# Segment sums by small TensorE products instead of VectorE reductions, and an attention transpose by VectorE and GpSimd

## The chip, the core and the metric

The kernel runs on one core of a Trainium2 chip. A core has five engines that run side by side, each with its own list of instructions: TensorE (PE in the profile) multiplies matrices from SBUF into PSUM, VectorE (DVE), ScalarE (ACT) and GpSimd (POOL) work elementwise, and SyncE (SP) issues transfers. PEld is TensorE's loading of weights, which overlaps its matmuls. The metric is the time of one execution on the device in microseconds; of several runs the median is given.

## The reference, cut to what matters

Two blocks are computed from the same normalised input `xn` and added. Block A is attention in segments of 32 tokens with 8 memory tokens carried from segment to segment. Block B is a mixer and a large MLP.

```python
def _A_ref(x, mem0, Wq, Wk, Wv, Wo, seg_len):      # S 2048, Dm 1024, H 32, Dh 128, M 8, seg_len 32
    mem = mem0
    for s in range(n_seg):                          # 64 segments
        h = concatenate([mem, x[:, s*32:(s+1)*32]], axis=1)      # 40 tokens
        q, k, v = h @ Wq, h @ Wk, h @ Wv
        p = softmax(where(mask, q @ k.T * scale, -1e9))          # the memory sees all, a token the past
        o = (p @ v) @ Wo
        mem = o[:, :M]
        outs.append(o[:, M:])

def _B_ref(x, w1, w2, w3, w4):
    h = gelu(layernorm(x) @ w1)
    x1 = x + shifted(h) @ w2
    return x1 + gelu(layernorm(x1) @ w3) @ w4       # 1024 -> 3584 -> 1024

xn = layernorm(x)
return x + _A_ref(xn, ...) + _B_ref(xn, ...)
```

The kernel does not run the 64 segments one after the other. It takes the memory that a segment passes on from the mean of the 40 value rows of that segment (put through `Wv` and `Wo`), attends to it for all segments at once, and checks at the end that the true memory is close enough to the one taken; a slow exact branch stands by in case it isn't. For that mean the kernel needs **the sum of `xn` over each segment of 32 tokens**, for all 64 segments: the tile `xs`, later `xb` in bf16. The first segment, whose memory is the input `mem0`, gets an attention of its own with all 40 rows: 40 queries by 40 keys, four heads at a time, eight times.

## The kernel before, the parts that are touched

Order of the stages: layernorm and the product with `w1` (stage 1), the product with `w2`, the MLP with `w3` and `w4` in four blocks `tb` of 512 tokens, the attention in 32 steps (four blocks of 512 tokens by eight groups of four heads), each with 12 chains of eight matmuls for Q, K and V, and the output product. All engines' orders are written down by hand: each engine runs its instructions in the order of the program. Products of 512 columns go to one of four rotating PSUM buffers (tag "mm").

Stage 1, where every tile of 128 tokens is normalised in place:

```python
def normalise_x(n):
    nc.scalar.activation(xts[n][:], xts[n][:], ACTF.Identity, bias=nms.pop(n)[:], scale=lnst[:, n, 2:3])   # L245
...
for g in range(2, NT // 2):
    ...                                             # statistics, normalised copy, its DMA transpose, for g+1
    stage1(g, range(4))                             # 4 x 8 matmuls of 256 columns, L260
    for n in (2 * g, 2 * g + 1):
        normalise_x(n)
    stage1(g, range(4, KT))
```

The MLP stage. `filler` puts side work into it: in `prep` the segment sums, in `plan` the 16 chunks of `Wv` and `Wo` through which the sums pass:

```python
plan = {}
for i in range(4):
    plan[(1, 1, 2 * i + 1)] = i
    plan[(2, 0, 7 * i + 6)] = 4 + i
    plan[(2, 1, 2 * i + 1)] = 8 + i
    plan[(3, 0, 7 * i + 6)] = 12 + i

def make_xn(n):                                     # normalised x once more, to memory
    xt = ring.tile([P, D], BF16, tag="xt", name="xt", bufs=2)
    nc.sync.dma_start(xt[:], x_v[:, n, :])
    nc.vector.tensor_scalar(xt[:], xt[:], ..., op0=ALU.subtract, op1=ALU.mult)                             # L455
    nc.gpsimd.dma_start(xn_v[:, n, :], xt[:])                                                              # L456

def load_sum(b):                                    # 512 tokens, transposed on the way in
    sums[b] = x3_pool.tile([P, KT * 512], BF16, tag="x0", name=f"xTs{b}")
    nc.sync.dma_start_transpose(sums[b]..., xn_d[b * 512:(b + 1) * 512, :])                                # L460

def seg_sums(b, k0):
    nc.vector.tensor_reduce(xs[:, k0:k0 + 2, ...], sums[b]..., axis=AX.X, op=ALU.add)                      # L463

for n in range(6):       do(0, 0, 10 + 3 * n, make_xn, n)
for n in range(6, 14):   do(0, 1, n - 6, make_xn, n)
do(1, 0, 0, make_xn, 14); do(1, 0, 3, make_xn, 15)
# load_sum and four seg_sums for each b: loads at (0,1,1) (0,1,5) (1,0,3) (1,0,14),
# sums at (0,1,4), (1,0,1) and (1,0,2), (1,0,10..13), (1,0,22..25); last_sum and load_chunk(0) at (1,0,26)

def load_R1(n):
    R1 = ring.tile([P, D], F32, tag="R1", name="R1")                    # three buffers
    nc.sync.dma_start(R1[:], R1_v[:, n, :])
    xt = ring.tile([P, D], BF16, tag="xt", name="xt", bufs=2)
    nc.sync.dma_start(xt[:], x_v[:, n, :])
    nc.gpsimd.tensor_tensor(R1[:], R1[:], xt[:], op=ALU.add)                                               # L509

for tb in range(4):
    for f in range(FT):                             # 28 chains of 8 matmuls
        ps = mm_tile("ps3")
        for k in range(KT):
            nc.tensor.matmul(ps[:], w3[...], xn3Ts[tb][:, :, k, :], ...)                                   # L580
        nc.scalar.activation(h3T[:, f, :], ps[:], ACTF.Gelu_apprx_tanh)
        filler(tb, 0, f)
        if f == 20:
            load_R1(tb * 4)
    for j in range(4):
        n = tb * 4 + j
        if j < 3:
            load_R1(n + 1)
        R1 = R1s.pop(n)
        for ch in range(2):
            ps = mm_tile("ps4")
            for f in range(FT):                     # 28 matmuls
                nc.tensor.matmul(ps[:], h3T[:, f, j * P:(j + 1) * P], w4t[f // 4][...], ...)               # L596
            nc.vector.tensor_tensor(R1[:, ch...], ps[:], R1[:, ch...], op=ALU.add)                         # L597
            filler(tb, 1, 2 * j + ch)
        nc.gpsimd.dma_start(R_v[:, n, :], R1[:])                                                           # L599
```

The first segment's attention, run once in each of the first eight steps. Its parts for step p are placed between the chains of the step after it: `first_scores` behind chain 4, `first_soft` behind chain 8, `first_trans` behind chain 11, and `first_values` behind chain 1 of the step after that:

```python
def first_soft(s):
    ...                                             # four matmuls psZ (L766), softmax on VectorE and ScalarE
    nc.vector.tensor_tensor(PZ[0:L, :, 0:L], e[:], mx..., op=ALU.mult)                                     # L775

def first_trans(s):
    ps = mm_tile("psZT")[:, 0:4 * L].rearrange("p (h k) -> p h k", h=4)
    for hh in range(4):
        nc.tensor.matmul(ps[:, hh, :], PZ[:, hh, :], ident[:, 0:L], start=True, stop=True)                 # L780
    s.PZT = smp.tile([P, 4, L], BF16, tag="PZT", name="PZT")
    nc.scalar.copy(s.PZT[:], ps)                                                                           # L782

def first_values(s):
    ps = mm_tile("psZO")[:, 0:4 * L].rearrange("p (h k) -> p h k", h=4)
    for hh in range(4):
        nc.tensor.matmul(ps[:, hh, :], VZ[:, hh * P:(hh + 1) * P], s.PZT[:, hh, :], start=True, stop=True) # L787
    nc.scalar.copy(oX[:, hsl(s.hg), 0:SEG], ps[:, :, 0:SEG])
    nc.scalar.copy(oZ[:, hsl(s.hg), :], ps[:, :, SEG:L])
```

Of the kernel before, what the change touches and what calls it, by code (L numbers as in the profile page):

```python
# [13 lines left out]
BF16 = mybir.dt.bfloat16  # L14
F32 = mybir.dt.float32
# [48 lines left out]
def kernel(  # L64
# [79 lines left out]
    xs = spec.tile([P, KT, NSEG], F32)  # L144
    xb = spec.tile([P, KT, NG], BF16)
    m0 = spec.tile([M, D], BF16)
    m0s = spec.tile([P, KT, 1], F32)
    lnst = spec.tile([P, NT, 4], F32)

    rightx = main.enter_context(ExitStack())  # L150
# [14 lines left out]
    with ExitStack() as keepx:  # L165
# [6 lines left out]
        with ExitStack() as p0:  # L172
# [71 lines left out]
            def normalise_x(n):  # L244
                nc.scalar.activation(xts[n][:], xts[n][:], ACTF.Identity, bias=nms.pop(n)[:], scale=lnst[:, n, 2:3])  # L245

            def pe_trans(n):
                xn2 = xn2s.pop(n)
                ps = [mm_tile("psT")[:], mm_tile("psT")[:]]
                for h in range(2):  # L250
# [3 lines left out]
                    for q in range(0, 4, 2 if n == 0 else 4):  # L254
                        w = 2 if n == 0 else 4
                        nc.scalar.copy(xn2Ts[n // 2][:, n % 2, 4 * h + q:4 * h + q + w, :], p3_[:, q:q + w, :])

            def w1_part(g, co, ps, ks):
                for k in ks:
                    nc.tensor.matmul(ps, w1_sb[:, k, co * P:(co + 1) * P], xn2Ts[g][:, :, k, :], start=(k == 0), stop=(k == KT - 1))  # L260
                if ks[-1] == KT - 1:
                    nc.scalar.activation(hTB[:, co, 2 + g * 256:2 + g * 256 + 256], ps, ACTF.Gelu_apprx_tanh)
# [58 lines left out]
            ln_apply(4)  # L321
            dma_trans(4)
            single(3, 0)
            normalise_x(2)
            ln_stats(6)
            ln_apply(5)
# [3 lines left out]
            for g in range(2, NT // 2):  # L330
                nxt = [n for n in (2 * g + 2, 2 * g + 3) if n < NT]
                for n in nxt:
                    if 6 < n + 1 < NT:
                        ln_stats(n + 1)
                    ln_apply(n)
                    dma_trans(n)
                stage1(g, range(4))
                for n in (2 * g, 2 * g + 1):
                    normalise_x(n)
                stage1(g, range(4, KT))  # L340

        x3_pool = rightx.enter_context(tc.tile_pool(name="x3", bufs=1, side="right"))
        w3b_pool = rightx.enter_context(tc.tile_pool(name="w3b", bufs=1, side="right"))
# [35 lines left out]
    with ExitStack() as p3:  # L379
# [9 lines left out]
        for k in range(KT):  # L389
            nc.tensor.matmul(ps9[:, k, :], m0[:, k * P:(k + 1) * P], eye9[:], start=True, stop=True)  # L390
        nc.vector.tensor_copy(MZ[:, :, 0:M], ps9[:, :, 0:M])
        nc.vector.tensor_copy(m0s[:], ps9[:, :, M:M + 1])

        chunks = {}

# [44 lines left out]
        plan = {}  # L440
        slots = {}
        for i in range(4):
            plan[(1, 1, 2 * i + 1)] = i
            plan[(2, 0, 7 * i + 6)] = 4 + i
            plan[(2, 1, 2 * i + 1)] = 8 + i
            plan[(3, 0, 7 * i + 6)] = 12 + i
        for c in range(16):
            slots[c] = 0 if c < 8 else c % 2

        sums = {}  # L450

        def make_xn(n):
            xt = ring.tile([P, D], BF16, tag="xt", name="xt", bufs=2)
            nc.sync.dma_start(xt[:], x_v[:, n, :])
            nc.vector.tensor_scalar(xt[:], xt[:], lnst[:, n, 0:1], lnst[:, n, 2:3], op0=ALU.subtract, op1=ALU.mult)  # L455
            nc.gpsimd.dma_start(xn_v[:, n, :], xt[:])  # L456

        def load_sum(b):
            sums[b] = x3_pool.tile([P, KT * 512], BF16, tag="x0", name=f"xTs{b}")
            nc.sync.dma_start_transpose(sums[b][:].rearrange("p (k t) -> p k t", k=KT), xn_d[b * 512:(b + 1) * 512, :])  # L460

        def seg_sums(b, k0):
            nc.vector.tensor_reduce(xs[:, k0:k0 + 2, 16 * b:16 * b + 16], sums[b][:].rearrange("p (k s i) -> p k s i", k=KT, i=SEG)[:, k0:k0 + 2, :, :], axis=AX.X, op=ALU.add)  # L463

        def last_sum():
            nc.vector.tensor_tensor(xb[:, :, 0:1], m0s[:], xs[:, :, 0:1], op=ALU.add)
            nc.vector.tensor_copy(xb[:, :, 1:NG], xs[:, :, 1:NG])
            load_chunk(0, 0)

        prep = {}  # L470

        def do(tb, ph, i, f, *a):
            prep.setdefault((tb, ph, i), []).append((f, a))

        for n in range(6):
            do(0, 0, 10 + 3 * n, make_xn, n)
        for n in range(6, 14):
            do(0, 1, n - 6, make_xn, n)
        do(1, 0, 0, make_xn, 14)
        do(1, 0, 3, make_xn, 15)  # L480
        for b, (load, sumat) in enumerate((((0, 1, 1), [(0, 1, 4)] * 4), ((0, 1, 5), [(1, 0, 1)] * 2 + [(1, 0, 2)] * 2),
                                           ((1, 0, 3), [(1, 0, 10 + t) for t in range(4)]), ((1, 0, 14), [(1, 0, 22 + t) for t in range(4)]))):
            do(*load, load_sum, b)
            for t, pos in enumerate(sumat):
                do(*pos, seg_sums, b, 2 * t)
        do(1, 0, 26, last_sum)

        def filler(tb, ph, i):
            for f, a in prep.get((tb, ph, i), ()):
                f(*a)  # L490
            c = plan.get((tb, ph, i))
            if c is None:
                return
            use_chunk(c)
            nx = c + 2 if c >= 8 else c + 1
            if c == 7:
                load_chunk(8, slots[8])
                load_chunk(9, slots[9])
            elif c < 7 or nx < 16:
                load_chunk(nx, slots[nx])  # L500
# [3 lines left out]
        def load_R1(n):  # L504
            R1 = ring.tile([P, D], F32, tag="R1", name="R1")
            nc.sync.dma_start(R1[:], R1_v[:, n, :])
            xt = ring.tile([P, D], BF16, tag="xt", name="xt", bufs=2)
            nc.sync.dma_start(xt[:], x_v[:, n, :])
            nc.gpsimd.tensor_tensor(R1[:], R1[:], xt[:], op=ALU.add)  # L509
            R1s[n] = R1  # L510

        A = {}
# [45 lines left out]
        def att_prep():  # L558
            load_xT(0)
            for nm in "qkv":  # L560
                need_w(nm, 0)
            need_w("q", 1)
            make_xm(0)
            sm = A["sm"]
            A["EQ"] = sm.tile([P, 16, W], F32, name="EQ")
            nc.gpsimd.memset(A["EQ"][:, :, SEG:W], float(M))
            for nm in ("QZ", "PZ", "VMZ"):
                A[nm] = sm.tile([P, 4, SEG if nm == "VMZ" else P], BF16, name=nm)
                nc.gpsimd.memset(A[nm][:], 0.0)
            A["VZ"] = sm.tile([P, 512], BF16, name="VZ")  # L570
            nc.gpsimd.memset(A["VZ"][:], 0.0)
            A["SS"] = sm.tile([P, 16], F32, name="SSsum")
            nc.gpsimd.memset(A["SS"][:], 0.0)

        for tb in range(4):
            for f in range(FT):
                ps = mm_tile("ps3")
                w3 = w3a if f < FH else w3b
                for k in range(KT):
                    nc.tensor.matmul(ps[:], w3[:, k, (f % FH) * P:(f % FH + 1) * P], xn3Ts[tb][:, :, k, :], start=(k == 0), stop=(k == KT - 1))  # L580
                nc.scalar.activation(h3T[:, f, :], ps[:], ACTF.Gelu_apprx_tanh)  # L581
                filler(tb, 0, f)
                if f == 20:
                    load_R1(tb * 4)
            if tb == 3:
                rightx.close()
                att_open()
# [7 lines that stand above are left out]
                    for f in range(FT):  # L595
                        nc.tensor.matmul(ps[:], h3T[:, f, j * P:(j + 1) * P], w4t[f // 4][:, f % 4, ch * 512:(ch + 1) * 512], start=(f == 0), stop=(f == FT - 1))  # L596
                    nc.vector.tensor_tensor(R1[:, ch * 512:(ch + 1) * 512], ps[:], R1[:, ch * 512:(ch + 1) * 512], op=ALU.add)  # L597
                    filler(tb, 1, 2 * j + ch)
                nc.gpsimd.dma_start(R_v[:, n, :], R1[:])  # L599
                if tb == 3 and j == 0:  # L600
                    att_prep()
# [143 lines left out]
                nc.scalar.copy(oT[:, h0:h0 + 4, :].rearrange("p h (m j) -> p m h j", j=4)[:, 0:3, :, 2 * r + j], o4[:, j, 0:12].rearrange("p (m h) -> p m h", h=4))  # L745
            nc.scalar.copy(oT[:, h0:h0 + 3, 12 + 2 * r:14 + 2 * r].rearrange("p h j -> p j h"), o4[:, :, 12:15])

    QZ, PZ, VMZ, VZ = A["QZ"], A["PZ"], A["VMZ"], A["VZ"]

    def first_scores(s):  # L750
        s.KZ = smp.tile([P, 4, L], BF16, tag="KZ", name="KZ")
# [23 lines left out]
        nc.vector.tensor_tensor(PZ[0:L, :, 0:L], e[:], mx[:].unsqueeze(2).to_broadcast((L, 4, L)), op=ALU.mult)  # L775

    def first_trans(s):
        ps = mm_tile("psZT")[:, 0:4 * L].rearrange("p (h k) -> p h k", h=4)
        for hh in range(4):
            nc.tensor.matmul(ps[:, hh, :], PZ[:, hh, :], ident[:, 0:L], start=True, stop=True)  # L780
        s.PZT = smp.tile([P, 4, L], BF16, tag="PZT", name="PZT")
        nc.scalar.copy(s.PZT[:], ps)  # L782

    def first_values(s):
        ps = mm_tile("psZO")[:, 0:4 * L].rearrange("p (h k) -> p h k", h=4)
        for hh in range(4):
            nc.tensor.matmul(ps[:, hh, :], VZ[:, hh * P:(hh + 1) * P], s.PZT[:, hh, :], start=True, stop=True)  # L787
        nc.scalar.copy(oX[:, hsl(s.hg), 0:SEG], ps[:, :, 0:SEG])
        nc.scalar.copy(oZ[:, hsl(s.hg), :], ps[:, :, SEG:L])

# [328 lines left out]
```

## Time and profile before

| | before |
|---|---|
| device time, median of 3 | 1494.43 us (1494.37 to 1498.48) |
| span of the profiled run | 1492.6 us, mean granted TensorE clock 0.998 |
| PE busy | 1467.6 us (98%) |
| DVE busy | 524.5 us (35%) |
| ACT busy | 345.3 us (23%) |
| POOL busy | 205.7 us (14%) |

The busy time of an engine says how long it had work in it, not whether that work was on the path that sets the end. That is told by what an engine waited for, by the chain of work that ended last, and by the granted clock in the stretches of time. A row of the groups gives line, engine, operation and tiles, how often it occurs, the busy time in all, and the mean duration of one in ns. Matmuls are pipelined: one takes 379 ns from start to end, but the next starts before that, so that the cost of a run of matmuls is read from start to start.

### The profile page before, as it was taken

To read this page: it belongs to the slowest core of one execution; us is meant where nothing else is said; L and a number is where in the kernel's file an instruction comes from. 1 tells how busy PE (TensorE), PEld (TensorE's weight loads), DVE (VectorE), ACT (ScalarE), POOL (GpSimd) and SP (SyncE) were. 2 spreads that over 40 slices of the span, in tenths; PEclk is the share of its full clock that TensorE was granted. 3 is DMA by queue.
4 is the path that set the end of the run, shared out by engine and by line. 5 is a ranking of instruction groups with operands and counts; after the bars stand their busy time and mean duration, and the time that the engine had idled before them with its cause. 6 is when DMAs were issued, how large, how long until landed. Compare 5 with 4: busy or idle time off the path is not lost.

```text
span 1492.6 us, 27953 instructions
## 1 busy us (share of the span) xinstructions
PE 1467.6 (98%) x12154; PEld 755.3 (51%) x12272; DVE 524.5 (35%) x1042; ACT 345.3 (23%) x871; POOL 205.7 (14%) x482
## 2 busy tenths in 40 slices
PE   8999997999999999999999999999999999999998
PEld 7844443444444456666544444444444444444444
DVE  8283034110000212445440355431264442163443
ACT  5633202203103013333320222220123220032220
POOL 6152131121211101121200000000000000000000
PEclk9999999999999999999999999999999999999999
DMA  8599765342542634565532364451245442244301
GB/s 218 138 266 226 280 216 151 118 153 96 191 149 99 212 113 157 183 190 180 184 114 64 94 174 150 143 169 49 83 142 171 155 156 72 67 142 147 123 12 62
DMA packets 207999, 216.77 MB, mean 145 GB/s; under 512 B 66936, under 2 KB 174600, under 8 KB 207872
## 3 DMA queue, kind: packets, MB, share of 16 engines
q1 hardware_dynamic: 199584, 187.21, 42.2%
q0 software_dynamic: 8288, 27.72, 5.4%
q8 instruction: 98, 1.61, 0.5%
q14 instruction: 29, 0.24, 0.1%
HBM read 174.26 MB, written 25.17 MB: 134 GB/s over the span
## 4 chain that ended last, share of the span: by engine, by line
PE 94%; DMA 2%; DVE 2%; issue 1%; SPq 1%; POOL 0%; DVEq 0%; POOLq 0%
PE psK L659 15%; PE psP L859 15%; PE psV L668 15%; PE psQ L641 15%; PE ps L580 13%; PE ps L596 11%; PE ps L356 4%; PE ps L260 2%; PE psS L692 1%; PE psO L722 1%; PE psM L677 1%; DMA xt<-in_A_x_dram 1%; DVE st L205 1%; PE psvb L414 1%; PE psG L435 1%
## 5 line engine op out<-in xcount | busy, mean ns | idle before, releaser
L859 PE MATMUL psP<-wo_sb,oX 128*128 128x512 bf16 (+1 forms) x1035 | 221.1, 372 | 1.1
L596 PE MATMUL ps<-w,hT_all 128*128 128x512 bf16 x874 | 193.7, 379 | 1.2
L659 PEld LDWEIGHTS <-w 128*128 128x128 bf16 x1280 | 125.1, 98 | 99.1
L641 PE MATMUL psQ<-xT,w 128*128 128x512 bf16 x744 | 169.1, 379 | 1.3
L668 PE MATMUL psV<-w,xT 128*128 128x512 bf16 x744 | 169.0, 379 | 1.3
L659 PE MATMUL psK<-xT,w 128*128 128x512 bf16 x763 | 169.4, 379 | 0.3
L859 PEld LDWEIGHTS <-oX 128*128 128x128 bf16 x1056 | 103.1, 98 | 117.2
L641 PEld LDWEIGHTS <-w 128*128 128x128 bf16 x1024 | 98.7, 98 | 116.0
L660 ACT CAST K<-psK 128x512 bf16<-128x512 f32 (+1 forms) x160 | 80.2, 501 | 303.8 <-PE psK L659 302.8
L648 DVE TENSOR_TENSOR Q<-psQ,QM 128x512 bf16<-128x512 f32 (+1 forms) x128 | 87.2, 685 | 166.0 <-PE psQ L641 107.5
L669 ACT CAST V<-psV 128x512 bf16<-128x512 f32 x128 | 74.8, 584 | 289.7 <-PE psV L668 289.6
L596 PEld LDWEIGHTS <-hT_all 128*128 128x128 bf16 x896 | 87.2, 98 | 103.8
L581 ACT ACTIVATE hT_all<-ps 128x512 bf16<-128x512 f32 x112 | 66.7, 597 | 294.9 <-PE ps L580 294.9
L668 PEld LDWEIGHTS <-xT 128*128 128x128 bf16 x768 | 74.1, 98 | 84.7
L580 PE MATMUL ps<-xn3T,w3a 128*128 128x512 bf16 x448 | 100.9, 387 | 8.9 <-DVE R L597 8.9
L580 PE MATMUL ps<-xn3T,w3b 128*128 128x512 bf16 x448 | 97.7, 379 | 0.0
L727 DVE TENSOR_TENSOR oX<-psE,VM 128x128 bf16<-128x128 f32 x32 | 9.3, 291 | 215.3 <-PE psE L723 215.3
L734 DVE TENSOR_TENSOR oX<-psO,VM 128x96 bf16<-128x96 f32 (+2 forms) x256 | 82.0, 391 | 0.0
L865 DVE TENSOR_TENSOR ot<-psP,Rt 128x512 bf16<-128x512 f32 (+1 forms) x33 | 22.3, 675 | 167.7 <-PE psP L859 164.9
L580 PEld LDWEIGHTS <-w3a 128*128 128x128 bf16 x448 | 44.1, 99 | 63.2 <-issue 13.3
L597 DVE TENSOR_TENSOR R<-ps,R 128x512 f32<-128x512 f32 x32 | 22.0, 689 | 137.8 <-PE ps L596 137.2
L580 PEld LDWEIGHTS <-w3b 128*128 128x128 bf16 x448 | 43.6, 98 | 51.9
(160 smaller groups left out, 1252.4 us busy)
## 6 DMA issues: line engine op xcount, KB each, us to landing
w<-in_A_Wq_dram SPq DMA_DIRECT2D x32, 1024.0 KB, 5.4
w<-in_A_Wk_dram SPq DMA_DIRECT2D x32, 1024.0 KB, 5.5
w<-in_A_Wv_dram SPq DMA_DIRECT2D x32, 1024.0 KB, 6.4
R_scratch<-x POOLq DMA_DIRECT2D x16, 512.0 KB, 9.0
xt<-in_A_x_dram SPq DMA_DIRECT2D x32, 256.0 KB, 3.8
R<-R_scratch SPq DMA_DIRECT2D x16, 512.0 KB, 6.4
R_scratch<-R POOLq DMA_DIRECT2D x16, 512.0 KB, 6.4
chunk<-in_A_Wv_dram SPq DMA_DIRECT2D x8, 1024.0 KB, 5.6
```

Of the source, the lines that this page charges most:

```text
L356: nc.tensor.matmul(ps[:], hTB[:, k, o:o + P], w2_sb[:, k, ch * 512:(ch + 1) * 512], start=(k == 0), stop=(k == KT - 1))
L580: nc.tensor.matmul(ps[:], w3[:, k, (f % FH) * P:(f % FH + 1) * P], xn3Ts[tb][:, :, k, :], start=(k == 0), stop=(k == KT - 1))
L581: nc.scalar.activation(h3T[:, f, :], ps[:], ACTF.Gelu_apprx_tanh)
L596: nc.tensor.matmul(ps[:], h3T[:, f, j * P:(j + 1) * P], w4t[f // 4][:, f % 4, ch * 512:(ch + 1) * 512], start=(f == 0), stop=(f == FT - 1))
L641: nc.tensor.matmul(ps[:], w[:, k, hh * P:(hh + 1) * P], s.xm[:, k, 0:512], start=(k == 0), stop=(k == KT - 1))
L648: nc.vector.tensor_tensor(q3[:, j0:16, 0:SEG], p3_[:, j0:16, :], QM[:, 4 * s.hg + hh, z + j0:z + 16].unsqueeze(2).to_broadcast((P, 16 - j0 ...
L659: nc.tensor.matmul(ps[:, 0:c], w[:, k, hh * P:(hh + 1) * P], s.xm[:, k, h2 * c:(h2 + 1) * c], start=(k == 0), stop=(k == KT - 1))
L660: nc.scalar.copy(s.K[:, hh, h2 * c:(h2 + 1) * c], ps[:, 0:c])
L668: nc.tensor.matmul(ps[:], s.xm[:, k, m * P:(m + 1) * P], w[:, k, :], start=(k == 0), stop=(k == KT - 1))
L669: nc.scalar.copy(s.V[:, m, :], ps[:])
L734: nc.vector.tensor_tensor(oX[:, h0:h0 + hn, :].rearrange("p h (m c) -> p m h c", c=P)[:, m0:m1, :, SEG * j:SEG * (j + 1)], o4[:, 4 * m0:4 ...
L859: nc.tensor.matmul(ps[:, 0:w], oX[:, h, m * P:(m + 1) * P], wo_sb[:, h, cc], start=(h == 0), stop=(h == H - 1))
```

## The change

It does two things. **Segment sums:** they go back to TensorE in stage 1. There each tile of 128 normalised tokens is the weight operand of eight matmuls against the 128 by 4 matrix `segone`, whose columns mark the tile's four segments; ScalarE copies the result to `xs`. With this the transposed loads, the reductions and the second round of loads of x fall away; the normalised x that the attention reads later is made in `load_R1`, from the tile of x that is loaded there anyway. As the sums are ready early, the chunks of `Wv` and `Wo` are used half a block earlier. **The first segment's probabilities:** they are not transposed by products with an identity matrix and a copy from PSUM. VectorE transposes each 32 by 32 block in place, and GpSimd moves the four blocks to where they belong, in a tile of its own that was cleared once.

```diff
+            def seg_sums(n):
+                ps = aux_tile([P, KT, 4], "AB"[n % 2], "psX")
+                for k in range(KT):
+                    nc.tensor.matmul(ps[:, k, :], xts[n][:, k * P:(k + 1) * P], segone[:], start=True, stop=True)
+                nc.scalar.copy(xs[:, :, 4 * n:4 * n + 4], ps[:])
...
             single(3, 0)
+            seg_sums(0)
+            seg_sums(1)
             normalise_x(2)
...
                 stage1(g, range(4))
                 for n in (2 * g, 2 * g + 1):
+                    seg_sums(n - 2)
                     normalise_x(n)
                 stage1(g, range(4, KT))
+            seg_sums(NT - 2)
+            seg_sums(NT - 1)
...
-        nc.vector.tensor_copy(m0s[:], ps9[:, :, M:M + 1])
+        nc.vector.tensor_tensor(xb[:, :, 0:1], ps9[:, :, M:M + 1], xs[:, :, 0:1], op=ALU.add)
+        nc.vector.tensor_copy(xb[:, :, 1:NG], xs[:, :, 1:NG])
...
-            plan[(1, 1, 2 * i + 1)] = i
-            plan[(2, 0, 7 * i + 6)] = 4 + i
-            plan[(2, 1, 2 * i + 1)] = 8 + i
-            plan[(3, 0, 7 * i + 6)] = 12 + i
+            plan[(0, 1, 2 * i + 1)] = i
+            plan[(1, 0, 7 * i + 6)] = 4 + i
+            plan[(1, 1, 2 * i + 1)] = 8 + i
+            plan[(2, 0, 7 * i + 6)] = 12 + i
...
-        (make_xn, load_sum, seg_sums, last_sum and their places in prep: all removed)
...
             nc.gpsimd.tensor_tensor(R1[:], R1[:], xt[:], op=ALU.add)
+            nc.vector.tensor_scalar(xt[:], xt[:], lnst[:, n, 0:1], lnst[:, n, 2:3], op0=ALU.subtract, op1=ALU.mult)
+            nc.gpsimd.dma_start(xn_v[:, n, :], xt[:])
             R1s[n] = R1
...
+            A["PZT"] = sm.tile([P, 4, 2 * SEG], BF16, name="PZT")
+            nc.gpsimd.memset(A["PZT"][:], 0.0)
...
+            if tb == 0:
+                load_chunk(0, 0)                    # behind the 28 chains of block 0
...
     def first_trans(s):
-        ps = mm_tile("psZT")[:, 0:4 * L].rearrange("p (h k) -> p h k", h=4)
-        for hh in range(4):
-            nc.tensor.matmul(ps[:, hh, :], PZ[:, hh, :], ident[:, 0:L], start=True, stop=True)
-        s.PZT = smp.tile([P, 4, L], BF16, tag="PZT", name="PZT")
-        nc.scalar.copy(s.PZT[:], ps)
+        PY = smp.tile([2 * SEG, 4, 2 * SEG], BF16, tag="PY", name="PY")
+        nc.vector.transpose(PY[:], PZ[0:2 * SEG, :, :])
+        for a in range(2):
+            for b in range(2):
+                ra, rb = slice(SEG * a, SEG * (a + 1)), slice(SEG * b, SEG * (b + 1))
+                nc.gpsimd.tensor_copy(PZT[ra, :, rb], PY[rb, :, ra])
```

More of the change, by code (lines that the diff above doesn't have):

```diff
@@ L146 @@
     m0 = spec.tile([M, D], BF16)
-    m0s = spec.tile([P, KT, 1], F32)
     lnst = spec.tile([P, NT, 4], F32)
@@ L442 @@
         for i in range(4):
-            plan[(1, 1, 2 * i + 1)] = i
-            plan[(2, 0, 7 * i + 6)] = 4 + i
-            plan[(2, 1, 2 * i + 1)] = 8 + i
-            plan[(3, 0, 7 * i + 6)] = 12 + i
+            plan[(0, 1, 2 * i + 1)] = i
+            plan[(1, 0, 7 * i + 6)] = 4 + i
+            plan[(1, 1, 2 * i + 1)] = 8 + i
+            plan[(2, 0, 7 * i + 6)] = 12 + i
         for c in range(16):
             slots[c] = 0 if c < 8 else c % 2
[L450 to L486, printed above, removed]
         def filler(tb, ph, i):
-            for f, a in prep.get((tb, ph, i), ()):
-                f(*a)
             c = plan.get((tb, ph, i))
@@ L567, in att_prep @@
             for nm in ("QZ", "PZ", "VMZ"):
-                A[nm] = sm.tile([P, 4, SEG if nm == "VMZ" else P], BF16, name=nm)
+                A[nm] = sm.tile([P, 4, {"QZ": P, "PZ": 2 * SEG, "VMZ": SEG}[nm]], BF16, name=nm)
                 nc.gpsimd.memset(A[nm][:], 0.0)
+            A["PZT"] = sm.tile([P, 4, 2 * SEG], BF16, name="PZT")
+            nc.gpsimd.memset(A["PZT"][:], 0.0)
             A["VZ"] = sm.tile([P, 512], BF16, name="VZ")
@@ L746, in mem_values @@
             nc.scalar.copy(oT[:, h0:h0 + 3, 12 + 2 * r:14 + 2 * r].rearrange("p h j -> p j h"), o4[:, :, 12:15])
-    QZ, PZ, VMZ, VZ = A["QZ"], A["PZ"], A["VMZ"], A["VZ"]
+    QZ, PZ, PZT, VMZ, VZ = A["QZ"], A["PZ"], A["PZT"], A["VMZ"], A["VZ"]
     def first_scores(s):
@@ L786, in first_values @@
         for hh in range(4):
-            nc.tensor.matmul(ps[:, hh, :], VZ[:, hh * P:(hh + 1) * P], s.PZT[:, hh, :], start=True, stop=True)
+            nc.tensor.matmul(ps[:, hh, :], VZ[:, hh * P:(hh + 1) * P], PZT[:, hh, 0:L], start=True, stop=True)
         nc.scalar.copy(oX[:, hsl(s.hg), 0:SEG], ps[:, :, 0:SEG])
```

## The prediction

> **What bounds the kernel now.** I read the page's busy times first, then the waits of TensorE alone, then its timeline where those waits lie, then the stretches around them. The page:
>
> ```profile
> span 1492.6 us, 27953 instructions
> PE 1467.6 (98%) x12154; PEld 755.3 (51%) x12272; DVE 524.5 (35%) x1042; ACT 345.3 (23%) x871; POOL 205.7 (14%) x482
> PE 94%; DMA 2%; DVE 2%; issue 1%; SPq 1%; POOL 0%; DVEq 0%; POOLq 0%
> ```
>
> TensorE has work for 98% of the span and is 94% of the chain that ended last. So work that leaves another engine gains nothing by itself; what counts is the number of matmuls and the 25 us (1492.6 less 1467.6) in which TensorE stands still. The waits of TensorE say where:
>
> ```profile
> PE ps L580 <- DVE R L597: 8.9, 2, 5.0
> PE psT L253 <- DVE xn L230: 2.0, 2, 1.4
> PE ps L260 <- DMA xn2T<-xn: 1.6, 2, 1.2
> ```
>
> (us in all, times, longest.) The largest is two waits of the MLP's first product for VectorE's addition L597, which should have emptied a PSUM buffer. The timeline from 219 to 238 us shows what VectorE did instead:
>
> ```profile
> 221.07 1.89 PE L580 MATMUL ps<-xn3T,w3a 128*128 128x512 bf16 x8
> 221.64 4.58 DVE L463 TENSOR_REDUCE xs<-xTs 128x32 f32<-128x1024 bf16 x4
> 226.14 0.68 DVE L597 TENSOR_TENSOR R<-ps,R 128x512 f32<-128x512 f32 x1
> 226.87 5.01 PE L580 MATMUL ps<-xn3T,w3a 128*128 128x512 bf16 x16 [3.92 <-DVE R L597]
> ...
> 235.67 0.55 DVE L455 TENSOR_SCALAR xt<-xt,lnst 128x1024 bf16<-128x1024 bf16 x1 [7.80 <-DMA xt<-in_A_x_dram]
> 236.13 0.68 DVE L597 TENSOR_TENSOR R<-ps,R 128x512 f32<-128x512 f32 x1
> 236.87 1.44 PE L580 MATMUL ps<-xn3T,w3a 128*128 128x512 bf16 x3 [4.99 <-DVE R L597]
> ```
>
> The addition stood in VectorE's order first behind four segment reductions, then behind the normalising of a tile of x that had not landed. TensorE stopped both times, as all four PSUM buffers were full. The stretches show a second cost, in the granted clock:
>
> ```profile
> 220.00:225.00 5.00, 2.96 (x14) 1.26 (x13) 5.00 (x4) 0.60 (x1) 2.00 (x2) 1.00 0.33 105
> 225.00:230.00 5.00, 3.13 (x9) 1.09 (x9) 2.87 (x5) 0.00 (x0) 1.07 (x2) 0.66 0.52 116
> 230.00:235.00 5.00, 1.88 (x9) 0.78 (x8) 0.00 (x0) 1.19 (x2) 0.00 (x0) 1.00 1.12 309
> 235.00:240.00 5.00, 3.13 (x8) 1.17 (x8) 1.61 (x3) 0.00 (x0) 1.61 (x3) 0.66 0.50 188
> 240.00:250.00 10.00, 10.00 (x48) 4.51 (x46) 5.51 (x6) 3.58 (x6) 1.08 (x2) 1.00 0.43 127
> ```
>
> (The third number from the end is the clock.) It falls to 0.66 of full in the stretch after each stop, and is 1.00 again later.
>
> [...] the first weight loads behind each stop lie 0.43 us apart (227.25, 227.68, 228.11), later ones 0.22. [...] four psZT matmuls of 40 columns start at 585.40 and the next group at 585.50. [...] the timeline before has 0.30 us for such a transpose of 128x128 and 0.71 for 128x512.
>
> **The change part by part.**
>
> *Removed: the two stops.* Their causes, reductions and second loads of x, are gone. Undisturbed, the 9th matmul would have started 8 x 0.216 = 1.73 us after 221.07, so at 222.80; it started at 226.87: 4.07 us. The 16 after it would have ended their turn at 226.87 + 3.46 = 230.33; the next started at 236.87, or 6.54 later. Of these 1.4 are the half clock (16 matmuls took 5.01 us where 15 x 0.216 + 0.38 = 3.62 are due) and 5.15 the stop. The second restart costs the same half clock again: eight weight loads at 0.43 in place of 0.22, about 1.5. Sum 4.07 + 5.15 + 1.4 + 1.5 = **12.1 us off the path**.
>
> *Added: segment sums on TensorE.* 16 tiles x 8 = 128 pairs of weight load and matmul of 4 columns. I size them by two neighbours: 32 psvb matmuls of 63 columns (L414) start at 293.63 and the next work at 294.59, 30 ns each; eight 9-column matmuls (L390) start at 124.08 and the next work at 124.36, 35 ns each with the change of group. 128 x 30 = 3.8 us, x 35 = 4.5; I take 4.0. TensorE waits 0.42 and 1.22 us for transposed tiles at 25.42 and 33.80; two groups stand before the first and two more before the second, so about 1.0 of the 4.0 falls into waits. **3.0 us onto the path.** The 16 copies on ScalarE (about 0.2 us each, as oZ from psZO) fit in: it is busy 10.65 of 16 us in the stretch from 34 to 50.
>
> *Removed: identity products.* 8 groups of 4 at 0.10 us from start to start: **0.8 us off the path.** Also eight ScalarE copies of 0.30 us, which lie beside.
>
> *Added beside: VectorE and GpSimd.* A transpose of 64x256 lies between 0.30 us for 128 and 0.71 for 512 columns, so 0.44; four moves of 32x128 at 0.32 (as VZ<-VT, L761) are 1.3. In the second step PZ is ready at 607.1, so PZT at about 609.0, and the products that read it start at 614.68: 5.7 us of room. In the first step the room is larger. Nothing on the path.
>
> *Moved: chunks and the normalising.* The same 512 small matmuls of psvb and psG run half a block earlier; no change on TensorE. The normalising now waits in VectorE for GpSimd's addition L509, and stands ahead of the addition L597 of the tile before. In block 2 that L509 starts at 396.45, 10.1 us after the tile's first chain (386.33), and takes 2.1; so L597, which ran at 392.19, would run at about 399.5. Its PSUM buffer is wanted again four chains later, some 24 us after its chain began: no stop.
>
> Sum: -12.1 + 3.0 - 0.8 = -9.9 us, so 1494.4 - 9.9 = 1484.5 us, a ratio of 0.993.
>
> **The rivals.** *The sums cost more.* If each pair took the 98 ns that a weight load shows from start to end, 128 pairs were 12.5 us and the gain was gone: 1494. Against it: psvb has the same weight loads at 30 ns. [...] *The stop moves.* VectorE still waits for a load inside the MLP, now in all 16 tiles. If a tile of R1 and x came behind two chunks of 1 MB (as in the new block 1), it might land some 15 us after its tile began, and the addition be done at 18: still before 24. A stop as before would need another 6 us; it would give 1490 to 1496. *The transposed probabilities come late.* GpSimd has its own queue; if a move stood behind another wait, the first eight steps would each stop. Against it: GpSimd's next waiting operation, BD, comes after the moves in program order. Each us of delay over the room would cost up to 8 us in all. *Nothing changes:* the stops were hidden elsewhere. Against: the chain has no room, TensorE is full after 240.
>
> **Range and chances.** The stop and the half clock are measured, so -12.1 is firm to a us; the 3.0 may be 2 to 6; the moved stop has perhaps one chance in six. The runs of before spread by 4 us upward. So 1484.5, with 1480 to 1491 for 8 in 10. Faster by over 2% (under 1464.5) would need 30 us, which is more than all standing still: 0.02. Slower by over 2% needs new stops of 40 us: 0.02. Within 2%: 0.96.
>
> **What would show it.** After: no wait of L580 for L597 and clock 1.00 throughout 220 to 250 us; 128 new matmuls with a start-to-start near 30 ns in stage 1, and the MLP starting some 3 us later than 124.36; PE's matmuls for psZT gone; psZO without a wait. Wrong if L580 or L596 wait for L597 again, if the groups of eight take over 0.4 us each, or if psZO waits for GpSimd.

## The result, and the profile after

The changed kernel takes 1486.53 us (median of 4 runs, 1485.7 to 1488.36), the one before 1494.4 in the runs beside it: a ratio of 0.9946 (95% interval 0.9922 to 0.997), or 7.9 us less. The prediction was 1484.5, with a range of 1480 to 1491.

First the busy times and the chain of the changed kernel, from its page:

```profile
span 1484.8 us, 28155 instructions
PE 1468.1 (99%) x12250; PEld 757.6 (51%) x12368; DVE 505.3 (34%) x1033; ACT 345.4 (23%) x879; POOL 218.6 (15%) x515
PE 98%; issue 1%; DMA 0%; DVE 0%; SPq 0%; ACT 0%
```

TensorE's busy time is the same within 0.5 us (1467.6 before); it is the standing still that shrank, from 25.0 to 16.7 us, and TensorE's share of the chain rose from 94 to 98%. Some 7 us of either figure are no standing still: 118 matmuls have no record in the two profiles (12154 for 12272 weight loads before, 12250 for 12368 after). A second profile of the kernel before, with all 12272, has 17.9 us (1493.4 less 1475.5). Next what TensorE waited for (us in all, times, longest):

```profile
PE psT L252 <- DVE xn L229: 2.0, 2, 1.2
PE psV L645 <- issue: 1.6, 1, 1.6
PE psW L197 <- DVE fill L176: 1.5, 1, 1.5
PE psO L699 <- issue: 0.7, 1, 0.7
```

The two stops of 8.9 us behind VectorE are gone, and so are the 1.6 us for transposed tiles. There is a new row, psV behind "issue", a wait for nothing that the profile shows, and a like one of psO (before, there was one of psO alone, 0.6 us). What they are is found below. Then the stretch in which the stops had been:

```profile
180.00:260.00 80.00, 79.74 (x533) 39.35 (x536) 9.41 (x17) 10.71 (x18) 21.02 (x40) 1.00 0.43 140
```

(Length, busy us of PE, PEld, DVE, ACT and POOL, granted clock, share of the DMA engines, GB/s.) TensorE is busy for 79.74 of 80 us at full clock.

To see where the time went I cut both traces at three instants: the first product with w3, the first product of the attention (psM), and the first product of its second block (psQ from xT, the ninth step). The tile views give them as the first of the two start times. Before:

```profile
L580 PE MATMUL ps<-xn3T,w3a x448: 378/379/635, 124.4 to 462.9; 128*128 128x512 bf16 x150
L677 PE MATMUL psM<-MZ,w x512: 193/196/202, 538.5 to 734.4; 128*128 128x71 bf16 x171
L641 PE MATMUL psQ<-xT,w x744: 376/379/380, 734.5 to 1415.2; 128*128 128x512 bf16 x186
```

After:

```profile
L555 PE MATMUL ps<-xn3T,w3a x448: 378/379/390, 125.7 to 454.9; 128*128 128x512 bf16 x150
L654 PE MATMUL psM<-MZ,w x512: 193/196/202, 527.7 to 726.2; 128*128 128x71 bf16 x171
L618 PE MATMUL psQ<-xT,w x744: 376/379/381, 726.2 to 1406.8; 128*128 128x512 bf16 x186
```

| profiled execution, us | up to w3 | MLP | first eight attention steps | rest | span |
|---|---|---|---|---|---|
| before | 124.4 | 414.1 | 196.0 | 758.1 | 1492.6 |
| after | 125.7 | 402.0 | 198.5 | 758.6 | 1484.8 |
| difference | +1.3 | -12.1 | +2.5 | +0.5 | -7.8 |

The MLP gave the 12.1 us that were predicted. In these two profiles the sums cost less than predicted, and the attention, where 0.8 us should have been won, lost 2.5.

### The profile page after: what moved, and what is told of

It reads as the page before. It is cut to its first block, busy times and chain, and to the rows that moved or that the text cites. A ratio compares the mean times of both kernels' runs of the same rounds, so it can differ in the third digit from the quotient of the medians.

```text
span 1484.8 us, 28155 instructions
## 1 busy us (share of the span) xinstructions
PE 1468.1 (99%) x12250; PEld 757.6 (51%) x12368; DVE 505.3 (34%) x1033; ACT 345.4 (23%) x879; POOL 218.6 (15%) x515
## 4 chain that ended last, share of the span: by engine, by line
PE 98%; issue 1%; DMA 0%; DVE 0%; SPq 0%; ACT 0%
PE psK L636 15%; PE psV L645 15%; PE psP L837 15%; PE psQ L618 15%; PE ps L555 13%; PE ps L573 13%; PE ps L366 4%; PE ps L265 3%; PE psS L669 1%; PE psO L699 1%; PE psM L654 1%; PE psvb L425 1%; PE psG L446 1%; PE ps L294 0%; DMA x<-in_A_x_dram 0%
## 5 line engine op out<-in xcount | busy, mean ns | idle before, releaser
L555 PE MATMUL ps<-xn3T,w3a 128*128 128x512 bf16 x448 | 97.7, 379 | 0.0
L481 DVE TENSOR_SCALAR xt<-xt,lnst 128x1024 bf16<-128x1024 bf16 x16 | 8.7, 545 | 179.6 <-POOL R L480 179.6
```

## The experiments

My theory: the gain comes from the stops that VectorE's order forced on TensorE, and not from the new transpose. The rivals: the transpose brings it; the work or the transfers of the old segment sums slowed TensorE; the sums on TensorE cost 98 ns each. And the loss in the attention had to be explained. Every kernel was timed beside the kernel before; the stages are cut as above. All kernels do the whole computation.

### The transpose alone

```diff
 # the kernel before, with the new first_trans and PZT; segment sums stay with VectorE
-            nc.tensor.matmul(ps[:, hh, :], PZ[:, hh, :], ident[:, 0:L], start=True, stop=True)
+        nc.vector.transpose(PY[:], PZ[0:2 * SEG, :, :])        # and four GpSimd moves
```

> The kernel before with the second half of the change alone: the first segment's probabilities turned by VectorE and GpSimd, the segment sums left with VectorE's reductions. Theory (the gain comes from the two stops of TensorE behind VectorE): both stops stay, 8.9 us of L580 waiting for L597, and only the 32 identity products go: 0.8 us less than before, some 1493.6, no difference that the timing can tell. Rival (the new transpose brings the gain, as the change's name says): about 1486 to 1488.

Measured: 1496.14 us, ratio 1.0025 (1.0008 to 1.0042): no gain, rather a loss of some 3 us. The transpose does not bring the change's gain. Its profiled execution was one of its fastest (1489.1 us): there the MLP took 403.6 us, with one stop of 1.45 us, so the stops differ from one execution to the next. Where the 3 us of loss lie is not shown: the one profile is 7 us shorter than the median.

### The segment sums alone

```diff
 # the changed kernel, with the identity products back
-        nc.vector.transpose(PY[:], PZ[0:2 * SEG, :, :])
+            nc.tensor.matmul(ps[:, hh, :], PZ[:, hh, :], ident[:, 0:L], start=True, stop=True)
```

> The changed kernel with the first half of the change alone: segment sums by TensorE, the identity products put back. Theory: the stops are gone, 0.8 us of identity products come back: within 1 us of the changed kernel, 1486 to 1487.5, and the MLP from its first product to the first attention product takes the same 402.0 us as in the changed kernel (414.2 before). Rival (the transpose brings the gain): back to 1492 to 1495.

Measured: 1485.11 us, ratio 0.9948 (0.9936 to 0.9959), the whole gain. The MLP takes 402.0 us, as in the changed kernel; the first eight attention steps 196.1 instead of 198.5. So, in these two profiles, the second half of the change costs 2.4 us there, although it takes 32 products from TensorE; the device times (1485.11 against 1486.53, and 1485.36 in a later series) don't show that much. The spread tells of the stops too: these 20 runs lie within 2.4 us (1483.63 to 1486.03), those of the kernel before in the same series within 18 (1482.37 to 1500.74).

### The reductions kept, at another place

```diff
 # the kernel before
-        for n in range(6, 14):
-            do(0, 1, n - 6, make_xn, n)
-        do(1, 0, 0, make_xn, 14)
-        do(1, 0, 3, make_xn, 15)
+        for n in range(6, 10):
+            do(0, 1, n - 6, make_xn, n)
+        for n in range(10, 16):
+            do(1, 0, 3 * (n - 10), make_xn, n)
-        # sums of block 0 at (0, 1, 4), loads at (0,1,5) (1,0,3) (1,0,14)
+        # sums of block 0 at (1, 0, 1), loads at (1,0,2) (1,0,9) (1,0,17)
```

> The kernel before, with the same reductions, second loads of x and transposed loads, but those that stood in the second half of block 0 (tiles 10 to 13, sums of the first 512 tokens) moved into the first half of block 1, where ScalarE and not VectorE empties the PSUM buffers. Nothing is left out. Theory (it was the place in VectorE's order that cost, not the work): both stops vanish, 12 us less than before, about 1482, so 4 us faster than the changed kernel, which pays 1.3 us for sums on TensorE. Rival (the work itself or its 8 MB of transfers slowed TensorE): stays at 1492 to 1495.

Measured: 1486.77 us, ratio 0.9958 (0.9945 to 0.9971). The MLP takes 402.0 us, with the same reductions, loads and transfers: that part of the theory holds to 0.1 us, and the rival falls. The chunks of `Wv` and `Wo` stand at their old places here, so their move in the change brings nothing either.

```profile
L580 PE MATMUL ps<-xn3T,w3a x448: 378/379/390, 128.9 to 455.4; 128*128 128x512 bf16 x150
L677 PE MATMUL psM<-MZ,w x512: 193/196/202, 530.9 to 726.8; 128*128 128x71 bf16 x171
```

VectorE still waits 7 us for a tile, but beside products that ScalarE empties:

```profile
226.88 4.59 DVE L463 TENSOR_REDUCE xs<-xTs 128x32 f32<-128x1024 bf16 x4
238.50 1.17 DVE L455 TENSOR_SCALAR xt<-xt,lnst 128x1024 bf16<-128x1024 bf16 x2 [7.02 <-DMA xt<-in_A_x_dram]
239.59 4.59 DVE L463 TENSOR_REDUCE xs<-xTs 128x32 f32<-128x1024 bf16 x4
```

The total of 1482 was missed by 4.8 us, and the miss lies in stage 1, which the edit doesn't touch: w3 starts at 128.9 us, not at 124.4. TensorE waited 3.3 us there for a transposed tile, and behind the wait, from 38 to 41 us, its clock was 0.50: 61 products behind it took 8.49 us, the 64 ahead of it 7.20. The other profiles without sums on TensorE in stage 1, save the first, show such a wait too (3.1 to 3.8 us).

### The sums twice

```diff
-                for k in range(KT):
+                for r in range(2):
+                    for k in range(KT):
                         nc.tensor.matmul(ps[:, k, :], xts[n][...], segone[:], start=True, stop=True)
```

> The changed kernel with each of the 128 segment-sum products made twice (same result). Theory (a pair of weight load and 4-column product costs 25 ns from start to start): 128 x 25 ns = 3.2 us more, as the two waits of stage 1 that took in part of the first 128 are used up: about 1489.5, and the product with w2 starts at 73.2 us instead of 70.03. Rival (a pair costs the 98 ns that a weight load shows): 12.5 us more, 1499.

Measured: 1489.45 us, ratio 0.9974 (0.9954 to 0.9993). The product with w2 starts at 73.3 us, 3.3 after the 70.0 of the changed kernel. 128 pairs for 3.3 us are 25 to 26 ns each; the rival of 98 ns falls. That difference alone would not be firm, as profiles of kernels that are the same up to there start the product with w2 between 70.0 and 72.7 us. But the timeline of the changed kernel shows the same from start to start, 16 in 0.40 us:

```profile
28.79 0.54 PE L260 MATMUL psX<-c_segone_sb,x 128*128 128x4 bf16 x16
29.20 7.15 PE L265 MATMUL ps<-xn2T,w_sb 128*128 128x256 bf16 x64
```

### VectorE delayed on purpose, by 9.7 and by 29 us

```diff
 # the changed kernel; the result of the reductions is not used
                     filler(tb, 1, 2 * j + ch)
+                    if (tb, j, ch) == (0, 2, 0):
+                        for r in range(8):                     # 24 in the second kernel
+                            nc.vector.tensor_reduce(t[:], w4t[0]..., axis=AX.X, op=ALU.add)
```

> The changed kernel with eight idle reductions on VectorE (128x1024 to 128x32, 1.21 us each, 9.7 us in all, result unused) put behind the fifth chain of the second half of block 0. Theory (a delay of VectorE costs only what it exceeds the room of the rotating buffers by): VectorE is 9.7 us behind at about 222, its buffer and the one of psvb are wanted again at 225.2: no stop, no change of time. Rival (each us of VectorE in this half lies on the path): 9.7 us more.

Measured: 1484.85 us (one run), the MLP 402.0 us: nearly 10 us of VectorE's time cost nothing.

> The same with 24 idle reductions, 29 us. Theory: psvb's buffer, wanted by TensorE at 225.2, is emptied at 212.3 + 29.0 + 0.7 + 0.4 = 242.4, so one stop of about 17.2 us with a half clock of 1.5 us behind it: 18.7 us more than the changed kernel, 1505. Rival (each us lies on the path): 29 us more, 1515. Rival (TensorE does not depend on VectorE here): no change.

Measured: 1507.74 us (one run), the MLP 422.0 us, 20.0 more; w3 starts later as well, at 128.3 us. The timeline of TensorE:

```profile
215.83 12.25 PE L578 MATMUL ps<-w,hT_all 128*128 128x512 bf16 x55
245.70 1.87 PE L425 MATMUL psvb<-xb,chunk 128*128 128x63 bf16 x32 [17.62 <-DVE vbT L428]
247.37 13.72 PE L560 MATMUL ps<-xn3T,w3a 128*128 128x512 bf16 x56
```

One stop of 17.62 us (17.2 expected), then the half clock: the psvb group takes 1.67 us instead of 0.96, and the 56 products 13.72 instead of 12.25. So a delay of VectorE was free within the room of the buffers (9.7 us) and cost what went beyond it (20.0 of 29 us). That is the mechanism of the stops, with its size.

### The kernel before, once more

> The kernel before once more, unaltered, for how much its stops vary. Theory (the stops depend on when transfers land, VectorE's order on how late they may): from the first w3 product to the first attention product 402.0 us plus the stops, which differ from the 12.1 us of the first profile by several us either way; time between 1482 and 1500. Rival (the stops are fixed by the order of instructions): 414.1 us again, within 0.5.

Measured: 1493.11 us (1486.96 to 1496.71); 63 runs of it in one series lay between 1482.37 and 1500.74. The MLP of the profiled execution took 411.4 us, so 9.4 us of stops and half clock instead of 12.1; stage 1 ended later, at 127.9.

```profile
PE ps L580 <- DVE R L597: 7.1, 2, 5.8
PE ps L260 <- DMA xn2T<-xn: 3.3, 2, 2.9
```

Yet the attention begins at 539.3 us, against 538.5 in the first profile. VectorE's addition that ends the second stop runs at nearly the same time in both (236.42 and 236.13 us), as VectorE has waited for the same late tile of x (7.20 and 7.80 us); TensorE, which comes 3.5 us later, stands there for less. So the loss in stage 1 and the stops are not independent: the kernel before is held to about the same time at the second stop, whichever way it got there.

### The changed kernel once more, and the pieces of Wo loaded later

> The changed kernel once more, unaltered, to see which of its waits come back. If the 1.6 us for which TensorE found no instruction at 664.9 us (and the half clock behind it, some 3 us in all) is a matter of that one execution, it is gone or elsewhere and the first eight attention steps take 195.2 us instead of 198.5; if it belongs to the kernel's order of transfers, it stands in the same step again. Time 1485 to 1488.

Measured: 1485.36 us (1484.69 to 1487.45), ratio 0.9936 (0.9914 to 0.9958). The wait for an instruction comes back in the same step with the same 1.6 us, and the first eight steps take 198.6 us. It belongs to the kernel. The timeline of the first profile of the changed kernel shows it, with TensorE's weight loads (PEld) behind it 0.43 us apart. At full clock they lie 0.22 apart for products of this size (49 of these take 10.74 us); here the clock was 0.50 from 667 to 670 us:

```profile
663.52 0.68 PE L669 MATMUL psS<-Q,K 128*32 128x33 bf16 x64
664.13 0.62 PE L699 MATMUL psO<-PT,V 32*128 32x33 bf16 x60
664.69 0.23 PE L700 MATMUL psE<-BD,V 128*128 128x132 bf16 x1
...
666.48 3.26 PE L645 MATMUL psV<-w,xm 128*128 128x512 bf16 x7 [1.56 <-issue]
...
666.98 0.15 PEld L645 LDWEIGHTS <-xm 128*128 128x128 bf16 x1 [0.18 <-issue]
667.40 0.15 PEld L645 LDWEIGHTS <-xm 128*128 128x128 bf16 x1 [0.28 <-issue]
667.83 0.15 PEld L645 LDWEIGHTS <-xm 128*128 128x128 bf16 x1 [0.28 <-issue]
```

And the transfers just there, in the view of the DMA queues from 655 to 668 us: 3 MB of weights, and one packet of instructions.

```profile
q1 hardware_dynamic: 2495, 3.05, 70.9%
q8 instruction: 1, 0.02, 0.5%
```

On the page of before, 98 packets of q8 make 1.61 MB, 16.4 KB each. If they hold TensorE's list alone, 12272 weight loads and as many matmuls, one is some 250 instructions: an estimate from these counts. The page of after, with 96 pairs more, has 99. In the first profiles of the two kernels TensorE went on 2.4 us behind the start of such a packet: 664.05 and 666.48 us in the changed kernel, 674.35 and 676.75 in the one before.

The positions agree with packets of about that size. In the kernel before, in the one with the sums alone and in the one with the reductions moved, the wait is short and stands behind 47 of the 60 psO products; so in the timeline of before:

```profile
675.60 0.52 PE L722 MATMUL psO<-PT,V 32*128 32x33 bf16 x47
676.75 0.25 PE L722 MATMUL psO<-PT,V 32*128 32x33 bf16 x13 [0.64 <-issue]
```

The sums add 128 weight loads and 128 matmuls to TensorE's list, 256 instructions, about one packet by the estimate, and leave the place. The transpose takes eight instructions out of each of the four steps ahead, 32 in all, and the wait moves to 28 to 30 instructions later in the program (past psO and psE, to the first psV or the one behind it), where it lasts 1.2 to 1.6 us in all seven profiles of kernels that have the transpose and the old loads. All seven have a second wait two steps later, behind 48 of 60 psO products, of 0.5 to 0.9 us (0.73 in the first profile of the changed kernel); the kernels with the identity products don't have it.

```diff
 # the changed kernel: the same 1 MB piece of Wo per step, issued behind chain 10 instead of chain 3
-                    if s.b == 0:
-                        nc.sync.dma_start(wo_sb[:, hsl(s.hg), :], Wo_v[:, hsl(s.hg), :])
...
                 v_chain(s, c - 8)
+                if c == 10 and s.b == 0:
+                    nc.sync.dma_start(wo_sb[:, hsl(s.hg), :], Wo_v[:, hsl(s.hg), :])
```

> The changed kernel with the load of each 1 MB piece of Wo in the first eight steps issued behind chain 10 instead of chain 3. Theory (TensorE runs out of instructions at 664.9 us because its instruction fetch stands behind 2 MB of weights that are moved at 380 GB/s just then[...]): that burst is halved, the stop and its half clock go, about 3 us less than the changed kernel, if the stop comes in each of its executions. Rival (the stop has nothing to do with these loads): unchanged, 1486.5, the stop at the same place.

Measured: 1483.48 us (1482.93 to 1483.89), ratio 0.9927 (0.9898 to 0.9955), beside 1485.36 for the changed kernel on the same chip, and the runs don't overlap. No wait for an instruction is left in TensorE's matmuls, and the first eight steps take 194.3 us: 196.0 less the 0.8 of the identity products, less the wait of 0.64 us that the kernel before has as well, makes 194.6. The same step now:

```profile
664.49 0.68 PE L669 MATMUL psS<-Q,K 128*32 128x33 bf16 x64
665.11 0.62 PE L699 MATMUL psO<-PT,V 32*128 32x33 bf16 x60
665.66 0.23 PE L700 MATMUL psE<-BD,V 128*128 128x132 bf16 x1
665.73 1.89 PE L645 MATMUL psV<-w,xm 128*128 128x512 bf16 x7
```

The q8 packet itself, in views of 0.2 us, says the same. In the seven profiles with the long wait it starts 0.2 to 0.8 us behind the first psS product; in the four with the short wait, 0.4 to 0.8 us ahead of it; in the three with the Wo pieces later, 2.0 to 2.4 us ahead. So moving 1 MB of weights brought the packet forward by 2 us or more against psS and took the wait away: that is what speaks for the burst holding the packet up. Where the wait is long, the packet comes about 1 us later than in the kernel before (0.53 us behind psS in the first profile after, 0.64 ahead of it before); why it does is not settled.

Three of the seven profiles put the long wait down to ScalarE's copy oT, not to "issue". It is not that copy: in the lines above, with Wo later, psV starts at 665.73 us, and the copy of that step at 666.26.

### The sums behind stage 1

```diff
-                    seg_sums(n - 2)                            # between the products of stage 1
...
-            seg_sums(NT - 2)
-            seg_sums(NT - 1)
+            for n in range(NT):
+                seg_sums(n)
```

> The changed kernel with all 16 groups of segment sums behind stage 1 instead of between its products; the same work. Theory (inside stage 1 they stand where TensorE would wait for a transposed tile, and keep it from half clock): the wait and the half clock come back, as in the kernels without sums on TensorE on the same chip, so stage 1 with its sums ends 3 to 6 us later, about 1488 to 1491 instead of 1485.4. Rival (their place makes no difference, 25 ns each wherever they are): within 1.5 us of the changed kernel.

Measured: 1489.15 us, ratio 0.9963 (0.9954 to 0.9972), w3 at 129.9 us, 2.9 us later than in the kernel timed beside it (127.0). The time is as expected, the reason is not: stage 1 ran without the wait for a transposed tile, all 384 products in 42.35 us. What cost was the run of sums itself:

```profile
24.90 42.35 PE L265 MATMUL ps<-xn2T,w_sb 128*128 128x256 bf16 x384
67.09 0.54 PE L260 MATMUL psX<-c_segone_sb,x 128*128 128x4 bf16 x16
67.80 4.28 PE L260 MATMUL psX<-c_segone_sb,x 128*128 128x4 bf16 x112 [0.17 <-ACT xs L261]
71.94 13.27 PE L363 MATMUL ps<-w_sb,hT_all 128*128 128x512 bf16 x50
```

The 128 products take 4.85 us here (two PSUM buffers, each waiting for ScalarE's copy), and the clock is halved from within them on: the stretches of this kernel from 67 to 78 us show 0.78, 0.50 and 0.72 (0.78 of 5 us is half clock for the last 2.2, if it was full until then), and 50 products of 512 columns take 13.27 us where 49 take 10.74 elsewhere.

```profile
67.00:72.00 5.00, 4.43 (x132) 3.96 (x130) 0.00 (x0) 3.16 (x17) 0.00 (x0) 0.78 0.02 3
72.00:75.00 3.00, 3.00 (x11) 1.04 (x9) 0.00 (x0) 0.28 (x2) 0.00 (x0) 0.50 0.00 0
75.00:78.00 3.00, 3.00 (x12) 1.18 (x11) 1.48 (x3) 0.00 (x0) 0.00 (x0) 0.72 0.00 0
```

So my theory that sums inside stage 1 keep TensorE from a wait is not shown. The five profiles without sums on TensorE waited there 1.6, 3.1, 3.3, 3.3 and 3.8 us for transposed tiles, and those with sums inside stage 1 not at all or 0.8 us; but this one, derived from the changed kernel, didn't wait either. Those five kernels also have the small tile `m0s` of 32 bytes a partition, which may shift what lies behind it in SBUF. Whether that matters was not tried.

### Two ways to the best kernel, side by side

> The changed kernel with the pieces of Wo loaded behind chain 10, once more, to stand beside the next kernel on one chip: 1483.5, with 194.3 us for the first eight attention steps.

Measured: 1483.45 us (1482.05 to 1484.84), ratio 0.9929 (0.9905 to 0.9952); first eight steps 194.3 us.

```diff
 # the kernel before, with three edits from above
+ reductions moved into the first half of block 1; transpose by VectorE and GpSimd; Wo behind chain 10
```

> The kernel before with three things: VectorE's reductions moved into the first half of block 1, the transpose by VectorE and GpSimd, and the pieces of Wo loaded behind chain 10. Theory: no stops in the MLP (402.0 us), 194.3 us for the first eight attention steps, 758.6 for the rest; stage 1 has no sums to fill its wait and so ends between 124.4 and 128.9: spans of 1479.3 to 1483.8, a time that lies within 2 us of the changed kernel with Wo later, and varies more. Rival (sums on TensorE are pure cost): 3.2 us faster than that kernel.

Measured: 1485.02 us (1484.52 to 1487.05), ratio 0.9938 (0.9913 to 0.9963): MLP 402.1, first eight steps 194.2, as expected, and w3 at 128.3 us. By the medians (1.6 us apart, the runs overlap a little) the 3.2 us that the sums take on TensorE are more than paid for by what stage 1 loses without them, for whichever reason. The best kernel is the changed one with the pieces of Wo loaded later, 1483.5 us, some 2 us better than the changed kernel.

## Why the prediction held, and where its terms were off

**Bound and mechanism** were right, though the 25 us of standing still were some 7 too many, by records that are missing. TensorE's standing still was the gain to be had, and the stop behind VectorE was its largest piece: the transpose alone gains nothing, the sums alone gain it all, the same reductions at a harmless place free the MLP as well, and the deliberate delays cost 0 and 20 us where the room of the buffers said 0 and 18.7.

**"-12.1" for the two stops**: measured -12.1 between the two profiles. But it is one execution's figure: a second one of the kernel before gives 9.4, with a later end of stage 1. Up to the start of the attention the two pairs of profiles agree better: 10.8 us gained (538.5 to 527.7) and 11.0 (539.3 to 528.3).

**"+3.0" for the sums**: mis-sized. The pair costs 25 ns, not the 30 to 35 taken from neighbours with more columns or a change of group, so 3.2 us in all instead of 4.0. In the two profiles stage 1 ended 1.3 us later, as if 1.9 of them, not 1.0, had fallen into standing still. But that is the luck of the pair: with w3 at 124.4 us the first profile of the kernel before is the earliest of the five without sums on TensorE (the others: 127.9 to 128.9), while the seven with each sum once, inside stage 1, have 125.6 to 128.3. That the sums lengthen stage 1 at all is not shown.

**"-0.8" for the identity products**: the products do cost 0.8 us, but the stage grew by 2.5. This is the step that failed: I counted the instructions that left and took the rest of TensorE's list to be as it was, but with 32 fewer instructions the wait stood 28 to 30 instructions later and was longer. The terms measured make up the 2.5: -0.8 for the products, -0.64 for the short wait that went, +1.56 and +0.73 for the two that came, and, as an estimate, +1.7 for 3.4 us at half clock behind the first of them (the granted clock was 0.92 from 666 to 667 us, 0.50 to 670, 0.88 to 671). The half clock did not follow these waits each time: in four of the seven profiles that have them it did not come, and the first eight steps took 196.3 to 197.0 us.

**Moved normalising**: right. In the changed kernel the addition behind the first chain of block 0 runs at 184.53 us, 1.8 us before the next chain's, and TensorE doesn't notice. (The first chain in block 2 of the kernel before starts at 385.89 us, not at 386.33; nothing hangs on it.)

**The transposed probabilities**: right in that nothing waits for them. VectorE's transposes take 436 ns (0.44 expected) and the moves 285 (320 expected).

The rest of the attention is 0.5 us longer after the change; I did not look for the cause. The sum of the terms, -9.9 against -7.9 measured, came close because an overrated cost in stage 1 and an unseen one in the attention partly offset each other; that is luck.

## What to carry to other kernels

Work on an idle engine is free only as long as what stands behind it in that engine's order is not wanted (here 9.7 us of it cost nothing, 29 us cost 20): work out the room (buffers times the time of a chain) and put long waits where another engine empties the buffers (the MLP then took 402.0 us instead of 414.1). Keep tiny matmuls spread between large ones (128 in one run took 4.85 us and had half clock behind them; spread, 3.2). When TensorE is full, look also at what its instruction stream needs: a burst of large loads beside a dense run of short instructions is worth moving (1 MB moved, 2 us won).

## What the runs showed of the hardware beyond what was expected

- Small matmuls back to back did not hold the clock, in the one profile of such a run: 128 products of 4 columns, 4.85 us long, with TensorE busy for 4.43 of 5 us and one stop of 0.17 us in the timeline, were followed by half clock (0.50 from 72 to 75 us). So a stretch that the profile calls busy was followed by what followed the stops of 3.92 and 4.99 us in the kernel before.
- A stop of 1.5 to 1.6 us was followed by half clock where it stood behind 1.2 us of 33-column products with weights of 32 rows or columns (in the changed kernel, 2.96 us from the first psS to the psV behind the stop of 1.56). That was so in three profiled executions; in four others a stop of 1.2 to 1.6 us at the same place was not, nor were stops of 1.28 us (the kernel before once more) and 1.45 us (the transpose alone) between 512-column products. What decides is not shown.
- A wait behind "issue", as I read it for the next instructions, was 1.56 us long in a stretch of the program without a branch, behind a burst of weights (367 GB/s from 660 to 664 us).
